# Transposing q and k of two batches by DMA instead of on TensorE, with earlier loads and an early exp table

## The chip, the cores and the metric

One core of a Trainium2 chip. The metric is the device time of one execution in microseconds (us), medians of several executions; executions of one kernel mostly differ by a few tenths of a per cent, at most by 1.5% (e10). Engines: TensorE (PE), VectorE (DVE), ScalarE (ACT), GpSimd (POOL), and SyncE (SP), which here only issues DMAs, in program order. In the profile lines L27 is the line of a helper through which every instruction is recorded, so go by the tile named ("ph", "po", "qT"): it is the one that the instruction writes. "x24" counts instructions, and "SPq" is SP issuing a DMA, a time that I call the hold.

## The reference, cut to what matters

Sparse attention (4 batches, 8 heads, 768 positions, head size 64: a local window, plus block maxima of k and block means of v), then a feed-forward layer over all 3072 tokens.

```python
k_sum = k.reshape(B, H, nb, block, D).max(axis=3)
v_sum = v.reshape(B, H, nb, block, D).mean(axis=3)
# scores_all: q . k in the window |i-j| < 16, and q . k_sum + log(block), both times 1/sqrt(D)
a = np.exp(scores_all - max);  a = a / sum
x = (a @ concat(v, v_sum)).transpose(0, 2, 1, 3).reshape(B * S, H * D)
h = x @ w_in                        # 512 -> 2048
g = h / (1 + np.exp(-1.702 * h))
out = g @ w_out                     # 2048 -> 512
```

## The kernel before

Work goes in eight rounds u = 0 to 7, each half a batch (384 tokens). A round's **input stretch** is 16 times `ff_in`, its **output stretch** 12 slots of `ff_out`; between the slots the attention of the next round is placed by a plan (s: scores of a head pair, v: values of two pairs, x: transposing their result, t: q of batch 1 transposed on PE).

```python
plan1 = {0: ["t0"], 1: ["t1"], 3: ["s0", "s1"], 4: ["t2"], 5: ["t3"],
         7: ["v0", "s2", "s3"], 8: ["x0"], 10: ["v1"], 11: ["x1"]}   # beside round 1's outputs
```

In the odd rounds k and q of the next batch (of batch 1 only k) are transposed on PE, between the `ff_in` of the round:

```python
def trans(src):                                    # six 128x128 transposes into PSUM ("ps_t")
    big = psb.tile([128, 2048], BF16, name="ps_t", tag="big")
    for j in range(NJ):
        pe.transpose(out=big[:, j * 128:(j + 1) * 128], in_=src[:, j], identity=ident)
def tk(p, s):                                      # k of head pair p
    ps = trans(...)
    dve.tensor_copy(out=..kx[p][s].., in_=ps)
    dve.tensor_reduce(out=ks, in_=ps..., op=ALU.max)
    key_halos(p, s); key_rows(p, s, ks)
def tq(p):
    dve.tensor_copy(out=qT[p], in_=trans(...))
```

The value side of a batch: `vsum` sums v over blocks on PE ("ps_vs"), `vrows` then sends halo rows and block sums into `vw` by six DMAs on SP, the **value rows**. The values of the next batch read them.

The softmax here doesn't subtract the row's maximum and nothing guards it: scores larger than these inputs give would overflow.

## Time and profile before

| | before |
|---|---|
| time, median of 3 (range) | 233.76 us (233.62 to 233.88) |
| span of the profiled execution | 232.1 us |
| PE busy | 218.1 us, 94% |
| ACT, DVE, POOL busy | 59%, 46%, 29% |

PE is busy nearly throughout and every other engine has room. How far the table can be trusted depends on the chain of waits: an engine that is busy 94% bounds the kernel only if its work follows itself without gaps. The prediction below shows those lines.

### The profile page before, as it was taken

How to read it: one execution, taken by the hardware profiler on the slowest of the kernel's cores; microseconds unless marked ns; L12 is line 12 of the kernel's file. 1: busy time of each engine (PE TensorE's matmuls, PEld its weight loads, DVE VectorE, ACT ScalarE, POOL GpSimd, SP SyncE). 2: the span in 40 equal slices, each digit the busy share in tenths (PEclk: the TensorE clock that was granted, in tenths of full speed). 3: DMA queues.
4: the chain of work that ended last, by engine and by line, in shares of the span. 5: the costliest groups of instructions: out<-in, count | busy, mean ns of one | idle time of the engine just before them, and what ended most of it. 6: DMA issues, size and time to landing. Idle time of an engine off the chain costs nothing.

```text
span 232.1 us, 5348 instructions
## 1 busy us (share of the span) xinstructions
PE 218.1 (94%) x2135; PEld 125.4 (54%) x2135; DVE 106.9 (46%) x288; ACT 137.2 (59%) x234; POOL 68.2 (29%) x164
## 2 busy tenths in 40 slices
PE   7578999989997999999999999999999999999992
PEld 4456665546554555556655555556655555555540
DVE  4889861546944700566926300758735301530000
ACT  3596768166647667645576378636567378727421
POOL 4477981147650014872000014862000000000000
PEclk9999999999999999999999999999999999999999
DMA  6999999999961199995131199995311200120021
GB/s 166 309 219 241 197 218 213 212 222 216 324 143 46 48 219 218 200 230 167 20 68 48 45 226 221 208 230 150 53 34 48 90 0 3 45 80 13 0 87 53
DMA packets 73305, 32.08 MB, mean 138 GB/s; under 512 B 57728, under 2 KB 70208, under 8 KB 73280
## 3 DMA queue, kind: packets, MB, share of 16 engines
q1 hardware_dynamic: 69056, 27.54, 53.0%
q0 software_dynamic: 4224, 4.19, 11.1%
q8 instruction: 17, 0.28, 0.5%
q14 instruction: 8, 0.07, 0.1%
HBM read 27.26 MB, written 6.29 MB: 145 GB/s over the span
## 4 chain that ended last, share of the span: by engine, by line
PE 83%; DVE 9%; ACT 3%; DMA 2%; issue 1%; SPq 0%; ACTq 0%; DVEq 0%
PE po L27 35%; PE ph L27 33%; PE ps_av L27 3%; DVE kx L27 3%; PE ps_t L27 3%; PE ps_s L27 3%; PE ps_x L27 2%; DMA kf<-in_k_dram 2%; DVE ks L27 1%; PE ps_k L27 1%; ACT kx L27 1%; PE ps_q L27 1%; DVE x_sb L27 1%; DVE xT L27 1%; PE ps_vt L27 1%
## 5 line engine op out<-in xcount | busy, mean ns | idle before, releaser
L27 PE MATMUL po<-w_out_sb,gT 128*128 128x512 bf16 x384 | 90.6, 380 | 0.0
L27 PE MATMUL ph<-xT,w_in_sb 128*128 128x384 bf16 x512 | 89.8, 326 | 0.8 <-DVE xT L27 0.6
L27 ACT ACTIVATE gT<-ph 128x384 bf16<-128x384 f32 x128 | 62.7, 491 | 32.5 <-PE ph L27 32.4
L27 PEld LDWEIGHTS <-w_in_sb 128*128 128x128 bf16 x512 | 48.5, 98 | 31.2 <-issue 1.4
L27 PEld LDWEIGHTS <-gT 128*128 128x128 bf16 x384 | 35.1, 98 | 36.6
L27 DVE TENSOR_TENSOR a_sb<-a_sb,mk 128x768 bf16<-128x768 bf16 x32 | 21.3, 677 | 57.8 <-ACT a_sb L27 56.8
L27 ACT ACTIVATE osb<-po 128x512 f32<-128x512 f32 x24 | 14.2, 596 | 38.1 <-PE po L27 32.5
L27 POOL CAST kb<-kf 128x768 bf16<-128x768 f32 (+1 forms) x13 | 10.5, 811 | 68.8 <-DMA kf<-in_k_dram 67.9
L27 ACT ACTIVATE a_sb<-ps_s 128x768 bf16<-128x768 f32 x32 | 24.4, 809 | 10.1 <-PE ps_s L27 9.9
L27 POOL CAST vw<-vf 128x768 bf16<-128x768 f32 (+3 forms) x35 | 26.1, 774 | 7.8 <-DMA vf<-in_v_dram 7.4
L27 ACT ACT_TABLE_LOAD x16 | 20.5, 1283 | 1.1 <-PEq L943 0.8
L27 DVE TENSOR_TENSOR x_sb<-ps_av,rc 128x384 bf16<-128x384 f32 x32 | 17.8, 558 | 1.1
L27 POOL CAST qb<-qf 128x384 bf16<-128x384 f32 (+1 forms) x18 | 11.4, 649 | 9.9 <-DMA qf<-in_q_dram 4.1
L27 DVE RECIPROCAL rc<-ps_av 128x6 f32<-128x6 f32 x32 | 6.1, 191 | 16.8 <-PE ps_av L27 16.8
L27 DVE COPY xT<-ps_x 128x768 bf16<-128x768 bf16 (+1 forms) x16 | 8.5, 531 | 7.0 <-PE ps_x L27 6.8
L27 DVE TENSOR_REDUCE ks<-ps_t 128x24 bf16<-128x768 bf16 x12 | 11.4, 948 | 0.0
L27 PEld LDWEIGHTS <-a_sb 128*64 128x64 bf16 x384 | 7.6, 111 | 6.3 <-issue 4.2
L27 DVE COPY kx<-kx 128x80 bf16<-128x80 bf16 (+4 forms) x52 | 9.2, 236 | 0.9 <-ACT kx L27 0.9
L27 PE MATMUL ps_av<-vw,a_sb 128*64 128x65 bf16 x384 | 9.5, 197 | 0.0
L27 DVE COPY kx<-ps_t 128x768 bf16<-128x768 bf16 x12 | 6.6, 552 | 6.1 <-PE ps_t L27 6.1
L27 PE MATMUL ps_x<-ident,x_sb 128*128 128x128 bf16 x96 | 8.7, 219 | 0.7 <-DVE x_sb L27 0.6
L27 PEld LDWEIGHTS <-kb 128*128 128x128 bf16 x96 | 7.9, 110 | 2.7 <-POOL vw L27 0.7
(68 smaller groups left out, 144.0 us busy)
## 6 DMA issues: line engine op xcount, KB each, us to landing
kf<-in_k_dram SPq DMA_DIRECT2D x32, 192.0 KB, 3.7
qf<-in_q_dram SPq DMA_DIRECT2D x32, 192.0 KB, 4.3
vf<-in_v_dram SPq DMA_DIRECT2D x32, 192.0 KB, 5.1
out_dram<-osb SPq DMA_DIRECT2D x24, 256.0 KB, 3.0
w_in_sb<-in_moe_w_in_dram POOLq DMA_DIRECT2D x4, 512.0 KB, 8.1
w_out_sb<-in_moe_w_out_dram POOLq DMA_DIRECT2D x4, 512.0 KB, 15.6
vw<-vs SPq DMA_DIRECT2D x6, 148.5 KB
vw<-vw SPq DMA_DIRECT2D x6, 99.0 KB, 2.9
```

The source lines that it names most:

```text
L27: r = f(*a, **kw)
```

## The change

Its intent is to take 16 groups of transposes off PE and put them on DMA engines, and to close two gaps at the ends of rounds 0 and 1. For the transposes to be in time, the loads are issued half a batch earlier; for that q needs a second set. In the traces ScalarE loads a table (16 loads of 1.28 us) when it changes between exp and gelu: `exp_soon()` is a tiny exp on an unused element ("the dummy"), there only to have the exp table loaded early, and `gelu_soon()` does the same for gelu.

```diff
+    def xk(p, s):
+        for e in range(2):
+            sp.dma_start(out=k4[:, :, e, e * 64:e * 64 + 64],
+                         in_=src[e * 64:e * 64 + 64], transpose=True)
+    def xq(p, s):
+        sp.dma_start(out=qT[p][s]..., in_=cast.pop(("q", p))..., transpose=True)
+    def rest_k(p, s):        # block maxima from kx in SBUF, halos, rows
...
+    def exp_soon():
+        act.activation(out=gate[:, 1:2], in_=gate[:, 0:1], func=ACT.Exp)
...  start of round 0
+    gelu_soon()
     copy(act, xT[0], ...); copy(act, xT[1], ...)
-    gelu_soon()
...  slots beside round 1's outputs, and round 0's
-    plan1 = {..., 3: ["s0", "s1"], ..., 7: ["v0", "s2", "s3"], 8: ["x0"], 10: ["v1"], 11: ["x1"]}
+    plan1 = {..., 2: ["s0", "s1"], ..., 6: ["v0", "s2", "s3"], 8: ["x0"], 9: ["v1"], 11: ["x1"]}
-    plan0 = {..., 6: ["x0"], 7: ["s3"], 10: ["v1"], 11: ["x1"]}
+    plan0 = {..., 6: ["x0", "s3"], 9: ["v1"], 11: ["x1"]}
...  rounds 2 and 4: casts, each followed by its transpose
+            for p in range(NP): cast_k(pool, p); xk(p, s)
+            for p in range(NP): cast_q(pool, p); xq(p, s)
+            for p in range(NP): cast_v(pool, s, p, 0); cast_v(pool, s, p, 1)
...  rounds 3 and 5
-            todo = {1: tk(0), 2: tk(1), 4: tk(2), 6: tk(3), 8: vsum(0..2), 9: vsum(3..5), vrows,
-                    10: tq(0), 11: tq(1), 13: tq(2), 14: tq(3)}
+            todo = {1: rest_k(0), 2: rest_k(1), 3: vsum(all), vrows, 5: rest_k(2), 7: rest_k(3)}
...  every round but the last, after its input stretch
+        if nxt: exp_soon()
...  loads of k, v, q of batches 2 and 3: in rounds 1 and 3, before in 2 and 4
```

More of the change, by code (lines that the diff above doesn't have):

```diff
@@ L180 @@
           for p in range(NP)]
-    qT = [keep.tile([128, S], BF16, name=f"qT{p}") for p in range(NP)]
+    qT = [[keep.tile([128, S], BF16, name=f"qT{p}_{s}") for s in range(2)]
+          for p in range(NP)]
     vw = [keep.tile([128, NQ, H, VC], BF16, name=f"vw{s}") for s in range(2)]
@@ L429, in q_copy @@
     def q_copy(p, eng, half=0):
-        copy(eng, qT[p][:, half * HALF:half * HALF + HALF].rearrange("p (c r) -> p r c", r=JH),
+        copy(eng, qT[p][0][:, half * HALF:half * HALF + HALF].rearrange("p (c r) -> p r c", r=JH),
              st["Q", p][:, 0:HALF].rearrange("p (r c) -> p r c", r=JH))
@@ L445, in score_tiles @@
                 pe.matmul(out=big[:, h * 512 + o:h * 512 + o + QT], lhsT=kx[p][s][r, i, :],
-                          rhs=qT[p][r, i * QT:i * QT + QT], start=True, stop=True)
+                          rhs=qT[p][s][r, i * QT:i * QT + QT], start=True, stop=True)
     def s_exp(p):
@@ L464, in b_turn @@
         pe.matmul(out=st["B", p // 2][r, 0:HALF], lhsT=ksz[:, p, :],
-                  rhs=qT[p][:, 0:HALF], start=True, stop=True)
+                  rhs=qT[p][0][:, 0:HALF], start=True, stop=True)
     def b_exp(g):
@@ L563, in tk @@
         key_rows(p, s, ks)
-    def tq(p):
-        ps = trans(cast.pop(("q", p)).rearrange("p r h d -> p r (h d)"))
-        dve.tensor_copy(out=qT[p], in_=ps)
+    def xk(p, s):
+        k4 = kx[p][s].rearrange("p (j e) c -> p j e c", e=2)
+        src = cast.pop(("k", p)).rearrange("p e r h d -> p (e r h d)")
+        for e in range(2):
+            sp.dma_start(out=k4[:, :, e, e * 64:e * 64 + 64],
+                         in_=src[e * 64:e * 64 + 64], transpose=True)
+    def xq(p, s):
+        sp.dma_start(out=qT[p][s].rearrange("p (j c) -> p j c", c=128),
+                     in_=cast.pop(("q", p)).rearrange("p r h d -> p (r h d)"), transpose=True)
+    def rest_k(p, s):
+        ks = attp.tile([128, nb], BF16, name="ks", tag="ks")
+        dve.tensor_reduce(out=ks.rearrange("p (j e n) -> p j e n", e=2, n=2),
+                          in_=at(flat_kx(p, s), 0, [[256, NJ], [192, 2], [block, 2], [1, block]]),
+                          axis=AX.X, op=ALU.max)
+        key_halos(p, s)
+        key_rows(p, s, ks)
     def tq1(p, eng):
@@ L576, in tq1 @@
                           rhs=ident, start=True, stop=True)
-        copy(eng, qT[p].rearrange("p (e c r) -> p e r c", e=2, r=JH),
+        copy(eng, qT[p][1].rearrange("p (e c r) -> p e r c", e=2, r=JH),
              big.rearrange("p (e x) -> p e x", e=2)[:, :, 0:HALF]
@@ L832 @@
     plan = {0: ["s0", "s1"], 4: ["v0", "s2", "s3"], 6: ["x0"], 8: ["v1"], 10: ["x1"]}
-    plan1 = {0: ["t0"], 1: ["t1"], 3: ["s0", "s1"], 4: ["t2"], 5: ["t3"],
-             7: ["v0", "s2", "s3"], 8: ["x0"], 10: ["v1"], 11: ["x1"]}
-    plan0 = {0: ["s0", "s1"], 4: ["v0", "s2"], 6: ["x0"], 7: ["s3"], 10: ["v1"], 11: ["x1"]}
+    plan1 = {0: ["t0"], 1: ["t1"], 2: ["s0", "s1"], 4: ["t2"], 5: ["t3"],
+             6: ["v0", "s2", "s3"], 8: ["x0"], 9: ["v1"], 11: ["x1"]}
+    plan0 = {0: ["s0", "s1"], 4: ["v0", "s2"], 6: ["x0", "s3"], 9: ["v1"], 11: ["x1"]}
     w51 = vw[1].rearrange("p (j e) h c -> p j e h c", e=2)
@@ L862 @@
                 todo[4 + p] = [lambda p=p: (q_turn(p, 1), q_copy(p, dve, 1))]
-        elif half == 1 and b + 1 < B:
-            s = (b + 1) % 2
-            todo = {1: [lambda: tk(0, s)], 2: [lambda: tk(1, s)],
-                    4: [lambda: tk(2, s)], 6: [lambda: tk(3, s)],
-                    8: [lambda: vsum(s, (0, 1, 2))],
-                    9: [lambda: vsum(s, (3, 4, 5)), lambda: vrows(s)],
-                    10: [lambda: tq(0)], 11: [lambda: tq(1)],
-                    13: [lambda: tq(2)], 14: [lambda: tq(3)]}
-            if u == 1:
-                todo = {2: [lambda: tk(0, s)], 4: [lambda: tk(1, s)],
-                        6: [lambda: tk(2, s)], 8: [lambda: tk(3, s)],
-                        14: [lambda: halo_odd(w51, 0), lambda: vsum(s, range(NJ))],
-                        15: [lambda: block_sums(), lambda: halo_even(w51, 0),
-                             lambda: sum_dmas(w51, 0)]}
-            cast_k(pool, 0)
-            cast_k(pool, 1)
-            cast_k(pool, 2)
-            cast_k(pool, 3)
+        elif u == 1:
+            s = 1
+            todo = {2: [lambda: tk(0, s)], 4: [lambda: tk(1, s)],
+                    6: [lambda: tk(2, s)], 8: [lambda: tk(3, s)],
+                    14: [lambda: halo_odd(w51, 0), lambda: vsum(s, range(NJ))],
+                    15: [lambda: block_sums(), lambda: halo_even(w51, 0),
+                         lambda: sum_dmas(w51, 0)]}
+            for p in range(NP):
+                cast_k(pool, p)
             for p in range(NP):
@@ L883 @@
                 cast_v(pool, s, p, 1)
-            if u == 1:
-                for p in range(NP):
-                    cast_q1(p)
-            else:
-                cast_q(pool, 0)
+            for p in range(NP):
+                cast_q1(p)
+        elif half == 0 and b + 1 < B:
+            s = (b + 1) % 2
+            for p in range(NP):
+                cast_k(pool, p)
+                xk(p, s)
+            for p in range(NP):
+                cast_q(pool, p)
+                xq(p, s)
+            for p in range(NP):
+                cast_v(pool, s, p, 0)
+                cast_v(pool, s, p, 1)
+        elif b + 1 < B:
+            s = (b + 1) % 2
+            todo = {1: [lambda: rest_k(0, s)], 2: [lambda: rest_k(1, s)],
+                    3: [lambda: vsum(s, range(NJ)), lambda: vrows(s)],
+                    5: [lambda: rest_k(2, s)], 7: [lambda: rest_k(3, s)]}
         if u == 1:
@@ L894 @@
             ff_in(u, nt)
-            if half == 1 and b + 1 < B and b:
-                if nt == 9:
-                    cast_q(pool, 1)
-                    cast_q(pool, 2)
-                if nt == 11:
-                    cast_q(pool, 3)
             for f in todo.get(nt, ()):
@@ L903 @@
         nxt = u + 1 < 2 * B
+        if nxt:
+            exp_soon()
         i = 0
@@ L913 @@
             i += 1
-            if half == 0 and b + 1 < B and i == 1:
-                if b == 0:
+            nb_ = 1 if u == 0 else b + 2 if half else B
+            if nb_ < B and i == 1:
+                if u == 0:
                     sp.dma_start(out=hold, in_=w_out_sb[0:16, NT - 5, 0:16])
-                load_k(b + 1, 0)
-                load_k(b + 1, 1)
-                load_k(b + 1, 2)
-                load_k(b + 1, 3)
-                load_v(b + 1)
                 for p in range(NP):
-                    if b == 0:
+                    load_k(nb_, p)
+                load_v(nb_)
+                for p in range(NP):
+                    if u == 0:
                         load_q(1, p, 0)
@@ L927 @@
                     else:
-                        load_q(b + 1, p)
+                        load_q(nb_, p)
 _INS = ['q', 'k', 'v', 'moe_w_in', 'moe_w_out']
```

## The prediction

> **What bounds the kernel now.** I read the page first (busy shares, the 40 slices), then the chain of waits in order of time, then TensorE's waits by cause, then the timeline of the DMA-issuing queue SP, because the change adds work there.
>
> The page: TensorE (PE) is busy 94% of the span, and after the first eighth its row is nines; nothing else passes 59%.
>
> ```profile
> PE 218.1 (94%) x2135; PEld 125.4 (54%) x2135; DVE 106.9 (46%) x288; ACT 137.2 (59%) x234; POOL 68.2 (29%) x164
> ...
> PE   7578999989997999999999999999999999999992
> ...
> PE 83%; DVE 9%; ACT 3%; DMA 2%; issue 1%; SPq 0%; ACTq 0%; DVEq 0%
> ```
>
> The work is eight rounds (half batches, 0 to 7). Each has an input stretch (16 tiles "ph", 64 matmuls) and an output stretch of 12 slots (four "po" matmuls each), with the next round's attention between the slots. In the chain of waits, 64 ph matmuls take 10.40 us (162 ns each) where nothing is mixed in, and rounds 3 and 5 have six-matmul transposes ("ps_t") mixed in. From round 3 (the chain from 104 us), with the undisturbed round 4 at the end:
>
> ```profile
> 105.33 1.30 PE ph L27 x8
> 106.63 0.34 PE ps_t L27 x6
> 106.96 0.65 PE ph L27 x4
> 107.61 0.34 PE ps_t L27 x6
> ...
> 112.52 0.28 PE ps_vs L27 x12
> 112.80 0.76 PE ph L27 x4
> ...
> 118.20 0.33 PE ps_t L27 x6
> 118.53 0.65 PE ph L27 x4
> 119.18 0.86 PE po L27 x4
> ...
> 132.44 10.40 PE ph L27 x64
> ```
>
> The reader is to see that the pieces join without a gap: every transpose is paid in full, 0.336 us per group, and what is removed from PE here shortens the run. The other place is the end of round 1, where the chain leaves PE:
>
> ```profile
> 69.39 1.28 ACT L27
> 70.67 0.01 issue
> 70.68 0.82 ACT a_sb L27
> 71.50 0.04 issue
> 71.54 0.50 PE ps_q L27 x6
> ...
> 80.23 0.57 DVE x_sb L27
> 80.80 0.05 issue
> 80.84 0.36 PE ps_x L27 x3
> 81.20 0.02 issue
> 81.22 0.57 DVE xT L27
> ```
>
> The 1.28 us on ScalarE (ACT) is the load of the exp table: it comes late, behind an output copy, so the exp that frees a PSUM buffer is late and PE's third q transpose waits 1.43 us for it. At the end two normalisations on VectorE (DVE) and a copy hold PE.
>
> **What the Trainium skill says.** (1) "VectorE: DVE Perf Modes", section "The three transpose paths": a 128x128 bf16 transpose takes 390 ns on TensorE and 1309 ns through the DMA crossbar. The trace has 219 ns for one PE record, but back to back only 0.336/6 = 56 ns of PE; so the DMA form is slower, and pays only because it runs elsewhere. (2) "DMA: Bandwidth & Descriptors", section "Latency and other measured facts": DMA transposes move 261 GB/s with a non-contiguous middle dimension, 350 to 400 when contiguous. No transfer of this trace is such a transpose. (3) The same page, "DMA Transpose (X-bar)": two transposing streams corrupt each other; here all are on SP, so none has to wait for another stream. (4) "ScalarE: Activation LUTs", section "What ACT_TABLE_LOAD costs": about 1283 ns plus 1380 ns of drain. The trace agrees on the load (16 of mean 1283 ns); the drain is not seen, the exp starts 0.01 us after the load above.
>
> **The change part by part.**
>
> Removed from PE: in batches 2 and 3, eight transpose groups each (four k, four q), 16 x 0.336 = 5.4 us. DVE loses sixteen PSUM copies of 0.55 us, which were beside the path. The max over k blocks (0.95 us) now reads SBUF and stays on DVE; in the first batch the same operation from SBUF took 0.86 us. The value sums ("ps_vs") join into one group of 24. Split, they cost 2 x 0.28, plus 2 x 0.11 in the ph group after (0.76 against 0.65). Joined, as round 1 has them, 0.45 + 0.11. So round 3's input stretch should go from 119.18 - 105.33 = 13.85 us to 10.40 + 0.56 = 10.96. Saved: 2.9 us, twice, **5.8 us**.
>
> The exp table is loaded by a dummy right after the last gelu of every round. In ordinary rounds the load already stood there, before the first exp, so nothing is gained; 0.2 us of ACT is added off the path. In round 1 it moves from 69.39 to about 65.1. It then delays ACT's copy of the first q transpose (66.6 to 68.1, before 65.8 to 67.25). Walking round 1's output stretch with the rows of the trace: three slots and two transpose groups end at 67.8; the scores, now at slot 2, wait for both q copies (68.1 on ACT, 68.45 on DVE), so they end near 68.9, a new stall of about 0.6; from there the third and fourth q groups find their buffers free, since the exps start at 68.5 and not 70.7; slot 9 carries the second values, two slots (1.73 us) now cover their normalisation, and only the last copy (about 0.4 us) is uncovered. The next round's ph resumes near 80.25 instead of 81.83: **1.6 us**.
>
> Round 0's end has the same normalisation gap (PE idle 0.35 us before the last transposes and 0.32 before ph); with the second values one slot earlier only the second stays: **0.35 us**.
>
> The gelu load of round 0 moves ahead of two copies. ACT had idled 1.78 us before the first of them, so 1.28 + 0.2 fit: nothing. The second q set only removes a write-after-read wait that the earlier writes would have had.
>
> Sum: 5.8 + 1.6 + 0.35 = 7.75 us, 233.76 to 226.0. For small new waits I allow 0.5: **226.5 us**, or 3.1% less.
>
> **Added, and whether it stays hidden.** Per batch, twelve DMA transposes on SP (eight of 96 KB for k, four of 192 KB for q), 1.57 MB; at 261 GB/s that is an estimate of 6 us of transfer. SP also issues everything else, in order. The timeline of its queue in the kernel before:
>
> ```profile
> 81.51 5.53 SPq L27 DMA_DIRECT2D kf<-in_k_dram  x8
> 87.08 8.56 SPq L27 DMA_DIRECT2D vf<-in_v_dram  x8
> 95.74 6.53 SPq L27 DMA_DIRECT2D qf<-in_q_dram  x8
> ```
>
> So 24 loads take 20.6 us. In the changed kernel they start after round 1's value-row transfers (67.7), end near 88, and round 1's three stores go at 88 to 90. Output buffers are three, next needed near 95: no stall. Then the twelve transposes. If each holds SP for 1.3 us (estimate, the skill's duration of a 128x128 one), they end near 106. After them come round 2's stores and the six value-row transfers of batch 2 (about 5 us to issue and 3 to land), needed by the values in slot 4 of round 3, near 119. 106 + 2 + 5 + 3 = 116: hidden with about 3 us to spare; it stays hidden up to some 1.6 us per transpose. The k pieces are wanted on DVE near 104.5, but PE needs their result only near 114.5 (round 3's slot 0), so DVE may wait some. The casts on GpSimd (POOL), now k, q, v, end near 99, before the sums want v at 106. Batch 3 has a few us more of slack.
>
> **Rivals.** (a) The DMA transposes hold SP or the DMA engines longer than I take: at 2.1 us each (25 us) the value rows land near 125 and PE stalls about 6 us in round 3 and some in round 5, eating nearly all: 230 to 235; at 4 us, slower, 245 or more. For it: the 1309 ns is for a sixth of a q transpose, and the two skill figures differ widely when extrapolated. Against: the bandwidth figure, and that the loads were moved ahead for just this. (b) The transposes keep up, but the earlier casts and loads disturb rounds 1 and 2, as by late stores blocking the output buffers: I find 4 us or more of slack, and 1 to 2 us would be lost. (c) PE time removed comes back as another bound (ACT or DVE at the slots): in round 4, which has no transposes today, PE joins without gaps, so rounds 3 and 5 should look like it. (d) The exp dummy hurts by delaying the q copy: up to 1 us, leaving 227.5.
>
> **Range and chances.** With (a) absent, which I hold three in four or better, the time is 225 to 228. With a mild (a), 228 to 232. So 8 in 10 for 224.8 to 229.8. Two per cent faster is 229.1: faster 0.81, within 2% 0.12, slower 0.07.
>
> **What would show it.** Right: no ps_t group after round 1; PE's instructions down by 96; input stretches of rounds 3 and 5 near 10.96 us; ph of round 2 resuming near 80.0; table load right after round 1's last gelu; SP's transposes ending before about 110 and the value rows landing before 119. Wrong: PE waits named for a DMA into kx, qT or vw, or for DVE's ks in rounds 3 and 5; SP's transposes taking over 2 us each; a waiting output copy for a late store; round 1's output stretch still near 17 us.

## The result, and the profile after

225.28 us median of 4 (224.72 to 226.54), against 233.72 of 4. The ratio is 0.9646 (95%: 0.9605 to 0.9687).

First the page of the changed kernel, its chain by engine. Before, DVE had 9% of the chain; now little is left but PE. Much of the 9% lay in the start and in round 1's inputs, which the edit does not touch.

```profile
PE 86%; DVE 4%; ACT 3%; DMA 2%; issue 2%; SPq 1%; ACTq 0%
```

The chain of waits in round 5 (start, duration, what). There is no "ps_t" left, one group of value sums, and the next stretch begins at 163.10:

```profile
152.14 2.60 PE ph L27 x16
154.74 0.45 PE ps_vs L27 x24
155.19 7.91 PE ph L27 x48
163.10 0.22 PE po L27
```

The input stretch is 163.10 - 152.14 = 10.96 us. The end of round 1 in the same view: the table load is gone from the chain, in its place a short wait for the second q copy on DVE, and at the end only one copy:

```profile
66.58 1.46 DVE qT L27
68.04 0.04 issue
68.08 0.35 PE ps_s L27 x12
...
79.42 0.57 DVE xT L27
79.99 0.04 issue
80.04 2.11 PE ph L27 x12
```

The DMA queue SP of the changed kernel (start, duration, engine, operation, what), between the loads of batch 2 and its value rows:

```profile
90.61 2.33 SPq L27 DMA_DIRECT2D out_dram<-osb  x3
93.04 11.17 SPq L27 DMA_TRANSPOSE kx<-kb  x8
104.30 5.23 SPq L27 DMA_TRANSPOSE qT<-qb  x4
109.62 1.50 SPq L27 DMA_DIRECT2D out_dram<-osb  x3
111.22 2.63 SPq L27 DMA_DIRECT2D vw<-vw  x4
113.94 1.72 SPq L27 DMA_DIRECT2D vw<-vs  x2
```

Each row follows the one before almost at once, so SP has become a chain of its own: 1.40 us per k transpose, 1.31 per q transpose. In this execution it even reached PE. The chain of waits in round 3:

```profile
113.94 0.86 SPq L27
114.86 5.07 DMA vw<-vs
119.93 0.14 issue
120.06 0.54 PE ps_av L27 x23
```

From the start of its issue (114.86) the last value row took 5.07 us to land, and the values waited for it. That is the only new wait of PE of consequence. One more new wait is on ACT, whose copy of an output had to wait until an earlier store freed its buffer:

```profile
95.09 0.60 ACT L27 ACTIVATE osb<-po 128x512 f32<-128x512 f32 x1 [1.38 <-DMA out_dram<-osb]
```

It cost PE nothing: the chain of this stretch is PE, without that wait.

To see where the time came from, I cut each profile's chain of waits into stretches. The start (up to the first output matmul) is left out: it ended between 36.3 and 38.6 us in the profiles of kernels with the same start, by chance of the first loads and of PE's first transposes. Durations in us, from the chain; the last four columns are experiments told below.

| stretch | before | changed | changed again (e1) | DMA part alone (e2) | slots and dummy alone (e3) | changed, no dummy (e4) |
|---|---|---|---|---|---|---|
| round 0, outputs | 14.75 | 14.12 | 14.12 | 14.74 | 14.12 | 14.12 |
| round 1, inputs up to the value sums | 11.45 | 10.93 | 10.93 | 11.17 | 11.15 | 11.73 |
| round 1, from there to round 2's inputs | 18.48 | 17.09 | 17.09 | 18.47 | 17.10 | 17.10 |
| rounds 2 and 3 | 50.61 | 48.44 | 47.71 | 47.71 | 50.62 | 47.71 |
| rounds 4 and 5 | 50.78 | 47.88 | 47.88 | 47.88 | 50.77 | 47.88 |
| rounds 6 and 7, to the last output copy | 44.50 | 44.51 | 44.50 | 44.50 | 44.51 | 44.50 |
| sum | 190.57 | 182.97 | 182.23 | 184.47 | 188.27 | 183.04 |

The first execution of the changed kernel lost 0.73 us in rounds 2 and 3 to the value rows; its repeat did not. The second row has a wait of a transpose for a DVE reduction that comes and goes between 0 and 0.8 us with no pattern that fits an edit; I count it as chance. The rows that the change was meant to shorten give 7.82 us from before to e1 (0.63, 1.39, 2.90 and 2.90).

### The profile page after: what moved, and what is told of

Its sections match the earlier page's. It is cut to its first block, busy times and chain, and to the rows that moved or that the text cites. A ratio compares the mean times of both kernels' runs of the same rounds, so it can differ in the third digit from the quotient of the medians.

```text
span 224.8 us, 5149 instructions
## 1 busy us (share of the span) xinstructions
PE 211.4 (94%) x2017; PEld 122.5 (54%) x2039; DVE 97.3 (43%) x272; ACT 138.0 (61%) x241; POOL 68.1 (30%) x164
## 3 DMA queue, kind: packets, MB, share of 16 engines
q0 software_dynamic: 4224, 4.19, 11.3%
## 4 chain that ended last, share of the span: by engine, by line
PE 86%; DVE 4%; ACT 3%; DMA 2%; issue 2%; SPq 1%; ACTq 0%
PE ph L27 37%; PE po L27 35%; PE ps_av L27 3%; PE ps_s L27 3%; PE ps_x L27 2%; DMA vw<-vs 2%; PE ps_k L27 2%; PE ps_w L27 2%; ACT kx L27 1%; DVE qT L27 1%; PE ps_q L27 1%; PE ps_vt L27 1%; DVE xT L27 1%; SPq L27 1%; ACT a_sb L27 1%
## 5 line engine op out<-in xcount | busy, mean ns | idle before, releaser
L27 PE MATMUL po<-w_out_sb,gT 128*128 128x512 bf16 x362 | 87.9, 379 | 2.0 <-issue 1.3
L27 PE MATMUL ph<-xT,w_in_sb 128*128 128x384 bf16 x512 | 86.8, 326 | 1.2 <-DVE xT L27 0.6
L27 PEld LDWEIGHTS <-w_in_sb 128*128 128x128 bf16 x512 | 49.3, 98 | 33.7 <-issue 1.1
L27 DVE TENSOR_TENSOR a_sb<-a_sb,mk 128x768 bf16<-128x768 bf16 x32 | 20.8, 665 | 63.1 <-ACT a_sb L27 62.2
L27 ACT ACT_TABLE_LOAD x16 | 20.5, 1283 | 1.1 <-PEq L962 0.8
L27 DVE RECIPROCAL rc<-ps_av 128x6 f32<-128x6 f32 x32 | 6.1, 189 | 16.4 <-PE ps_av L27 16.3
L27 DVE TENSOR_REDUCE ks<-kx 128x24 bf16<-128x768 bf16 x12 | 11.3, 941 | 1.4 <-ACT kx L27 1.4
L27 PEld LDWEIGHTS <-kx 64*128 64x128 bf16 x384 | 7.0, 95 | 4.7 <-issue 4.0
L27 PE MATMUL ps_s<-qT,kx 64*128 64x64 bf16 x384 | 9.2, 191 | 0.4 <-ACT qT L27 0.2
L27 PEld LDWEIGHTS <-warm 128*128 128x128 bf16 x71 | 6.0, 115 | 6.4 <-issue 4.8
L27 DVE CAST qT<-ps_q 128x384 bf16<-128x384 f32 (+1 forms) x8 | 7.7, 961 | 3.7 <-PE ps_q L27 3.7
```

The source lines that it names most:

```text
L27: r = f(*a, **kw)
```

## The experiments

Twelve kernels ran, in three groups, each group on one chip beside the kernel before (233.09, 233.54 and 233.40 us median of 11).

### The same again, and the parts apart

**e1: the changed kernel unedited.**

> The changed kernel once more, unedited. Theory: the gain is steady at 8.4 us and only the start varies; expected 224.5 to 226.0 us. In the changed kernel's first profile the first transposes ran at twice their usual time (1.48 us for six, where the other groups took 0.82 in the kernel before) and cost about 0.8 us; if that is chance, this profile shows 0.82 and a span near 223.5. The 0.5 us wait of TensorE for the value rows in round 3 should come again, because the DMA queue SP is a fixed chain. Rival: both belong to the changed kernel (slow start every time), or the wait is chance and is gone here.

224.79 us (224.30 to 225.11), ratio 0.9635. The first transposes ran at 0.82 us, the span is 222.6 us, and the wait for the value rows is gone: both were chance. The last value rows and the values of this execution:

```profile
111.47 1.72 SPq L27 DMA_DIRECT2D vw<-vs  x2
117.80 0.57 PE L27 MATMUL ps_av<-vw,a_sb 128*64 128x65 bf16 x24
```

SP began the last row at 112.38 and was done at 113.19. When it landed is not in this trace. Where PE waits for this row the chain shows it: 3.4 to 3.8 us after the start of its issue in e5, e8, e9 and e10, and 5.07 us in the first profile. By these figures the slack here is an estimate of 1.6 to 2.0 us, or 0.4 with a landing as late as the first. In the first profile SP also began its transposes later against PE (2.27 us later than here, while PE's outputs began only 1.50 us later). So whether PE waits changes from execution to execution.

**e2: only the DMA part.**

```diff
 plans, gelu load: as in the kernel before
-        if nxt: exp_soon()
```

> The DMA transposes, early loads and two q sets alone; slots, exp dummy and gelu load as in the kernel before. Theory (TensorE time is removed one for one): 5.8 us less than the kernel before, minus the 0.5 us wait for value rows, so about 228.3 us. Rival (the slots and the dummy are needed for the transposes to pay, or the DMA part gives back more elsewhere): 230 us or more. Other rival (nearly all of the gain is the DMA part): 226 us or less.

227.21 us, ratio 0.9742, about 6.0 us less than before (0.0258 of 233.09). The table: 2.9 us in each of the two pairs of rounds, nothing at the ends of rounds 0 and 1, where the late table load stands in the chain as in the kernel before. One for one, as the theory says, and without the wait that it allowed for.

**e3: only slots, dummy and gelu load, on the kernel before.**

```diff
 in the kernel before: new plan0 and plan1, exp_soon(), gelu_soon() ahead of the copies
```

> The kernel before with only the new slots, the exp dummy and the earlier gelu load; transposes stay on TensorE. Theory: the end of round 1 gives 1.4 us and the end of round 0 about 0.35, so about 232.0 us, and together with the DMA part alone this adds up to the whole. Rival (these parts were only to make room for the DMA part): 233.7 us, no gain.

230.77 us, ratio 0.9896, 2.4 us less. The table gives 0.63 at round 0's end, 1.38 at round 1's. The parts add up: 6.10 + 2.30 = 8.40 us, and the whole saves 8.34 in e1.

**e4: the changed kernel without the dummy exp.**

```diff
-        if nxt:
-            exp_soon()
```

> The changed kernel without the dummy exp. Theory A (the dummy is what brings the exp table early, as the change says): the wait of the third q transpose comes back, 1.0 to 1.4 us, so about 226.5 us. Theory B (putting the scores one slot earlier already places the first exp ahead of the output copy in ScalarE's order, so its table load comes early by itself): no loss, 225.0 to 225.4 us, and the new wait of the first scores for the q copy, 0.17 us in the profile, is gone or smaller.

225.36 us, ratio 0.9668 (0.9631 to 0.9704), an interval that includes e1's 0.9635. The times alone can't exclude a loss of some tenths of a us; the mean is raised by the profiled execution (227.31 us), whose start ran with a granted TensorE clock of 0.50 from 22.0 to 25.4 us. The stretch decides: round 1's end takes 17.10 us, as with the dummy (17.09), and rounds 2 to 7 are as in e1. Why is seen in the timeline of ACT without the dummy (start, duration, operation, what):

```profile
66.88 1.46 ACT L27 ACTIVATE qT<-ps_q 128x768 bf16<-128x768 f32 x1 [0.71 <-PE ps_q L27]
68.36 1.28 ACT L27 ACT_TABLE_LOAD   x1
69.66 1.51 ACT L27 ACTIVATE a_sb<-ps_s 128x768 bf16<-128x768 f32 x2
71.05 0.61 ACT L27 ACTIVATE osb<-po 128x512 f32<-128x512 f32 x1
```

With scores at slot 2 the exps stand ahead of the output copy ("osb") in ACT's order. The load is placed in front of the first exp, so it goes right after the q copy, while PE is still waiting for the other q copy on DVE, and the exps are done before the third transpose wants their buffer. Theory B holds: **with the new slot the dummy adds nothing.** It does move the load (64.69 us in the changed kernel), but the slot alone brings it early enough. The dummy alone, with the old slot, was not run. The small wait of the scores did not go, as I had added to B: it is now for DVE's copy of q alone. In the other rounds no time is lost without the dummy either (table).

### How much room SP has

**e5: each q transpose issued twice.**

```diff
-        sp.dma_start(out=qT[p][s]..., in_=..., transpose=True)
+        for _ in range(2):
+            sp.dma_start(out=qT[p][s]..., in_=src, transpose=True)
```

> The changed kernel with each of the eight q transposes issued twice (the second writes the same data): about 5.4 us more on SP per batch. Theory (in rounds 3 and 5 the chain on SP, transposes then stores then value rows, has under 1 us of slack to the values on TensorE): about 5 us of wait on vw<-vs in each of the two rounds, 235 us, ratio near 1.005 to the kernel before. Rival (the slack of some 3 us that the prediction gave is there, the wait seen once was chance): 2 to 2.5 us per round, 230 us. Other rival (TensorE does not hang on SP at all): 225 us.

246.84 us, ratio 1.0565: far more than any theory gave, because the edit did more than I meant. SP waited with the second write of a tile until the first had landed (12.7 us in eight waits, by its view of waits). SP's line for the q part of batch 2:

```profile
101.68 17.33 SPq L27 DMA_TRANSPOSE qT<-qb  x8
```

So 12 us were added per batch, not 5.4. PE waited 17.9 us for vw<-vs in the two rounds together. It shows that PE hangs on SP; it does not measure the slack. e9 and e10 do.

**e6: q of pairs 2 and 3 after the value rows.**

```diff
                 cast_q(pool, p)
-                xq(p, s)
+                if p < 2: xq(p, s)
...
-            todo = {..., 3: vsum, vrows(s), ...}
+            todo = {..., 3: vsum, vrows(s), xq(2, s), xq(3, s), ...}
```

> The changed kernel with the transposes of q pairs 2 and 3 issued after the value rows; they are wanted only four slots after pairs 0 and 1. SP sends the value rows about 2.7 us earlier. Theory: no wait for vw<-vs in any profile, the value rows are issued near 2.7 us earlier against the scores, time 224.3 to 225.2 us, steadier than the changed kernel but at most 0.5 us faster, since the wait is met only in some executions. Rival: q of pairs 2 and 3 now come late and TensorE waits for qT in slot 4: 226 us or more.

225.00 us (224.60 to 226.41), ratio 0.9641. No wait for value rows or q in the profile. SP sent the last value row at 111.95, and the values began at 118.46, 6.5 us later, where e1 had 4.6. No gain in time can be told from chance: the wait is met only sometimes.

**e7: value rows of batches 2 and 3 on GpSimd's queue.**

```diff
-        sp.dma_start(out=w5[...], in_=...)      # six of them, in vrows of rounds 3 and 5
+        pool.dma_start(out=w5[...], in_=...)
```

> The changed kernel with the value rows of batches 2 and 3 issued from GpSimd's queue instead of SP. Theory: they no longer stand behind the transposes, so they leave right after the value sums, several us earlier; no wait for them; 224.3 to 225.2 us. Rival (they land late because the loads behind share the engines, not because SP sends them late): landing stays near 5 us and the wait can come again.

224.51 us (224.07 to 226.22), ratio 0.9624. Those of batch 2 left by 108.02, 9.8 us before the values; they landed in 4.7 us (median over both batches, 3.7 to 5.9), the last of batch 2 at 112.45, 5.4 us before the values. So, as the rival says, they land no faster, but they leave early enough for it not to matter. The second half of the rival, that the wait can come again, is not seen in this one profile.

**e8: loads where they were before, the rest half a batch later.**

```diff
-            nb_ = 1 if u == 0 else b + 2 if half else B
+            nb_ = B if half else b + 1
-        casts and transposes of the next batch in rounds 2 and 4
+        in rounds 3 and 5, with vsum and vrows at ff_in 8, rest_k at 9, 11, 13 and 15
```

> The changed kernel with the loads where the kernel before had them, casts and transposes half a batch later (in the round that ends with their use). Theory: SP's chain of 24 loads, 12 transposes and 6 value rows, about 42 us, does not fit in one round and a half of room: scores wait about 5 us for q and values about 6 us more for their rows, twice: about 247 us, slower than the kernel before. Rival (the lead is only comfort, the transposes land within 3 us each): 226 to 228 us.

246.86 us, ratio 1.0544, slower than the kernel before by some 5%. PE's waits (engine and tile, waited for, us in total, times, longest):

```profile
PE ps_s L27 <- DMA qT<-qb: 8.5, 4, 3.9
PE ps_av L27 <- DMA vw<-vs: 5.6, 4, 1.6
```

These are the two waits expected, 14.1 us together. The rest of the 21 us over the changed kernel goes with a granted TensorE clock of 0.958 in the mean, of which more below. The edit also moves the value sums and puts v's casts before q's, so it tests this late schedule as a whole: without the lead of half a batch the DMA transposes did not pay.

**e9 and e10: two and four more, small, transposes per batch.** Each is 128x128 (32 KB) into a tile that nothing uses any more; so no landing is waited for.

```diff
         sp.dma_start(out=qT[p][s]..., in_=src, transpose=True)
+        if p < 2:                              # e10: 4
+            sp.dma_start(out=warm[:, p * 128:p * 128 + 128], in_=src[:, 0:128],
+                         transpose=True)
```

> The changed kernel with two more DMA transposes per batch on SP, each a sixth the size of a q transpose (128x128, 32 KB, into a tile that is dead by then), so nothing has to land before another. Theory: a transpose holds SP for a fixed 1.25 us whatever its size, so 2.5 us more per batch; slack to the values about 0.5 to 1 us over the two batches together; TensorE waits 4 to 5 us for vw<-vs in all, near 229.5 us. Rival A (the hold goes by bytes): 0.2 us each, no change, 225 us. Rival B (fixed hold, but 3 us of slack as predicted): 2 us in all, 227 us.

> As the two more, with four per batch. Theory: 5 us more per batch, 9 to 10 us of wait in all, 235 us, and a little more if the clock of TensorE falls in the long waits. Rival A: 225 us. Rival B: 7 us of wait, 232 us.

e9: 227.21 us, ratio 0.9747, 2.6 us more than e1 (0.0112 of 233.4). e10: 235.28 us, ratio 1.0046. How long each transpose held SP in e9 (ns, least, median, most):

```profile
L27 SPq DMA_TRANSPOSE qT<-qb x8: 1225/1238/2029, 103.1 to 159.3; - x8
L27 SPq DMA_TRANSPOSE warm<-qb x4: 1217/1226/1229, 104.4 to 156.6; - x4
```

A sixth of the bytes, the same hold: rival A falls. PE's waits in e9, in round 3 and in round 5:

```profile
118.84 0.19 PE L27 MATMUL ps_av<-vw,a_sb 128*64 128x65 bf16 x1 [0.26 <-DMA vw<-vs]
120.00 0.54 PE L27 MATMUL ps_av<-vw,a_sb 128*64 128x65 bf16 x23 [0.96 <-DMA vw<-vs]
...
168.47 0.19 PE L27 MATMUL ps_av<-vw,a_sb 128*64 128x65 bf16 x1 [0.55 <-DMA vw<-vs]
169.63 0.54 PE L27 MATMUL ps_av<-vw,a_sb 128*64 128x65 bf16 x23 [0.98 <-DMA vw<-vs]
```

These are 1.22 and 1.53 us. SP was given about 2.6 us per batch. So the slack was an estimated 1.4 us in round 3, and in round 5, if the doses of both batches minus the first wait add up (5.2 - 1.2 = 4.0), 2.5. Measured against e1 by the times (2.6 of 5.2 us), the same sum: **over both batches about 2.6 us of slack, varying by a us or two between executions.** I had expected 4 to 5 us of wait, so my figure for the slack was too small; rival B, 2 us in all and 227 us, came nearer. What the prediction gave for round 3 alone, 3 us, was still too much: the executions show -0.6 (the first of the changed kernel, which waited), 0.6 (e10: 5.1 us more of SP, 4.45 of wait), 1.4 (e9), and an estimated 1.6 to 2.0 (e1).

e10 waited 6.7 us but lost some 9.6 (0.0411 of 233.4 against e1). The rest is the clock. (In the profiled execution, the slowest of the four, rounds 2 to 5 took 11.3 us more than in e1.) The chain of waits in e10 after the wait of round 3:

```profile
124.50 3.53 PE po L27 x8
128.03 0.64 PE ps_x L27 x6
128.67 1.74 PE po L27 x8
```

Eight output matmuls take 3.53 us right after the wait and 1.74 four us later; the transposes between 0.64 instead of 0.34. From the first values to the next it is 7.5 us, in e9 after its shorter wait 4.9. So PE ran at half speed, which cost 2.6 us more; the trace has the granted clock at 0.50 from 121.7 to 128.6 us. In round 5 of e10 a wait of 0.86 and one of 1.38 us, with a single matmul between them, was enough (6.5 us instead of 4.9; the clock at 0.50 from 176.4 to 179.8). In e9, waits of 0.55 and 0.98 were not: its clock stayed at 1.00. The Trainium skill, "TensorE: Matmul & The Clock Gate", section "Why this matters for your kernels", asks for no idle gaps above about 3 us; the runs agree that long waits cost a slow restart, but in round 5 of e10 two shorter ones in a row did it too. No single limit follows from these runs: in the start of e4 the clock fell to 0.50 at 22.0 us, after a stretch (18.5 to 22.0) in which PE was busy for 1.98 us and no wait was over 1.02 us.

**e11: q of two head pairs in one DMA.**

```diff
-    four transposes of 192 KB: qT[p][s] <- q of pair p
+    two of 384 KB: qTT[g][s] <- q of pairs 2g and 2g+1, cast into one tile
```

> The changed kernel with q of two head pairs transposed by one DMA of 384 KB, so ten transposes per batch instead of twelve, the same bytes. Theory (fixed hold per instruction): the q part takes SP 2.6 us instead of 5.3, the value rows leave 2.7 us earlier, never a wait; 224.3 to 225.2 us. Rival (by bytes): the q part still takes 5.3 us and nothing changes.

224.91 us, ratio 0.9644. The hold of the double transposes:

```profile
L27 SPq DMA_TRANSPOSE qT<-qqb x4: 1451/1622/1853, 103.1 to 149.7; - x4
```

1.62 us for 384 KB against 1.24 for 192: neither theory whole. In these runs the hold is the same at 32, 96 and 192 KB (1.22 to 1.25 us, medians), and at 384 KB it is longer. The q part took 3.42 us of SP instead of 5.25, and no wait was seen.

**e12: value rows on GpSimd's queue, no dummy.**

```diff
 e7, and
-        if nxt: exp_soon()
```

> Value rows of batches 2 and 3 from GpSimd's queue, and no exp dummy: the parts of the change that the runs showed to pay, without the SP chain. Theory: as fast as the best so far, 224.2 to 225.0 us, ratio 0.960 to 0.963 to the kernel before, with no wait for vw<-vs. Rival: without the dummy something is lost after all (225.5 or more).

224.65 us (224.27 to 224.97), ratio 0.9628 (0.9606 to 0.9649). It beats the kernel before; from the changed kernel (0.9635 and 0.9646) it can't be told apart by time, but it has no wait for value rows, and is simpler by the dummy. The kernel after it in line would have to shorten PE's own work or the start.

## Why the prediction was right

225.28 us lies in the range (224.8 to 229.8), near its low end, and the repeat (e1, 224.79) just below it. 8.4 us were saved where the sum of steps said 7.75; the stretches that it names gave 7.82. That this is so near is partly luck: two small errors, at the ends of rounds 0 and 1, have opposite signs. The rest of the 8.4 lies outside them, in the start and in round 1's chance wait for DVE. Point by point:

- **PE's removed transposes are paid back one for one: right.** Rounds 3 and 5 were to have input stretches of 10.96 us; the profile has 10.96, and 2.9 us are saved in each (e2). It held because PE joined without gaps before, and the extra DMA work stayed beside it. So rival (c), another bound in these rounds, was not met.
- **Round 1's end: size near, cause half wrong.** Predicted 1.6 us, measured 1.39. The step "In round 1 it moves from 69.39 to about 65.1" credits the dummy; e4 shows that the new slot alone brings the load early enough, and beside it the dummy is worth nothing. I had read the load as late because nobody called it; it was late because an output copy stood ahead of the first exp.
- **Round 0's end: too small.** Predicted 0.35, measured 0.63: I left the wait for the last copy in full, yet with the work one slot earlier the whole gap shrank.
- **The gelu load: nothing, as said**, as far as can be seen beside a start that varies by 2 us.
- **SP stays hidden "with about 3 us to spare": the term was mis-sized.** The hold of 1.3 us per transpose was right (1.24 to 1.40 us), and so was the order of the chain. The slack in round 3 was between -0.6 and some 2 us. In e1 the rows were sent by 113.19, as the sum had it (113), but PE came to the values at 117.80 and not near 119 (0.75 us of that is its earlier start). In the first profile the rows were sent by 115.66, about 1 us later against PE than in e1, and the last row landed 4.3 us after the end of its issue; the 3 us of the sum fit the usual case (2.6 in e9). Batch 3 had no "few us more of slack": in e1 its rows were sent 4.7 us before their values, those of batch 2 4.6. Rival (a), which makes the kernel slower, was thus only some 0.4 us per transpose away (an estimate): e10, 5 us more of SP per batch of 12 transposes, undoes the whole gain.
- **Rivals (b) and (d): no cost seen.** The sign of (b) was there: an output copy waited for a late store, 1.38 us in the first profile and 0.8 to 1.2 in e6, e11 and e12, though the prediction had said "no stall". PE lost nothing by it: rounds 2 and 3 took 47.71 us in e6 and e12, and the same in e1, which had no such wait. So two of the prediction's own signs of being wrong, this one and a PE wait named for vw, did show in the first profile, at a cost of nothing and of 0.73 us. Of (d), the delayed q copy cost PE 0.17 us in the profile, inside the 0.6 us I had given the scores' wait.
- **The 0.5 us allowed for small waits** was met once (0.73 us in the first profile), and not in e1. The allowance is about half of the 1.2 us between 226.5 and 225.28; the other half is not traced beyond round 1's chance wait for DVE (0.5 us between the profiles) and the start.

## What to carry to other kernels

When one engine's chain has no gaps, work taken off it comes back one for one, as long as the queue that takes it over is counted as a chain too: write down what it issues, in order, with a hold per instruction and a landing at the end, and see when the last of it is wanted. A DMA transpose costs its queue by the instruction here, so few large ones, started well ahead, with urgent small transfers on another queue; here that bought room on SP (e7, e11), not time that could be told from chance. And before adding an instruction to pull a table load forward, look at what stands ahead of it in its engine's order; moving the user may do it for nothing.

## What the Trainium skill lacked or had wrong

- "VectorE: DVE Perf Modes", "The three transpose paths", gives 1309 ns for a 128x128 transpose by DMA. Here such a one held SP for 1.22 us, near that, but landed 2.4 us after its issue (e10, median), which is what a reader of the data waits for. The page has no dependence on size: 96 KB held SP 1.25 us, 192 KB 1.24, 384 KB 1.62, and landed in 2.9, 2.8 and 3.8 us (medians of the landings that the trace has; k and q of the changed kernel, and e11; in e10 q took 3.6).
- "DMA: Bandwidth & Descriptors", "Latency and other measured facts", gives 261 GB/s or more. At these sizes the hold of the queue binds: eight k transposes, 8 x 96 KB, took SP 11.17 us, which is 70 GB/s. The estimate of 6 us of transfer per batch made from that figure was of no use beside the 16.4 us that SP was held.
- "ScalarE: Activation LUTs", "What ACT_TABLE_LOAD costs": the 1283 ns of a load are in every trace; the 1380 ns of drain are not seen. After 15 of the 16 loads of each trace the next instruction starts within 12 ns (in e4 the load ends at 69.64 and the exp starts at 69.66); after the first load there are 1.25 to 1.40 us, in which ACT waits for the first k to land.
